# Rational layer: second product with tokens on the partitions, eight logit columns in the same product, inverse taken per block

## The chip, the cores and the metric

One core of one Trainium2 chip runs the whole program. The metric is device microseconds (us) of one execution. PE is the matrix engine, ACT, DVE and POOL the scalar, vector and general engines, SP the queue that issues most DMAs.

## What is computed

Three layers in a row on 8 × 3072 tokens of 256 channels. The first mixes along the sequence in the frequency domain; the second is the rational layer; the third routes every token to one of eight experts.

```python
# layer 2: x is the output of layer 1, 24576 x 256; w_in 256 x 2048, w_out 2048 x 256
h = x @ w_in
h2 = h * h
P = a[0] + a[1] * h + a[2] * h2 + a[3] * h2 * h
Q = 1.0 + np.abs(b[0]) * np.abs(h) + np.abs(b[1]) * h2
x = (P / (Q + 1e-06)) @ w_out
# layer 3: 8 experts, w1 256 x 1024, w2 1024 x 256
en = expert_emb / (norm(expert_emb) + 1e-06)
logits = (x / (norm(x) + 1e-06)) @ en.T / tau
e = argmax(logits); gate = softmax(logits)[e]
out = gate * (relu(x @ w1[e]) @ w2[e])
```

## The kernel before

Each layer is a stage. A planner (`list_order`, L83) simulates the engines with the costs of a table and writes one fixed order per engine: every engine then works off its list strictly in turn. Stage 1 and stage 2 have a list each.

**Stage 1** (`dft_phase`, L166) goes through 8 batches of 13 groups as matrix products. PSUM gives it two banks `pa`, shared by the first transform (`a_mm`, L264) and the last (`o_mm`, L412). Beside it run the `weight_steps` (L234): 32 chunks of `w_in` and `w_out` are read as float64, rebuilt on DVE (`w_bits`, L597 to 612) and split into a high and a low float32r part (`w_high`, `w_left`, `w_low`), which go back to DRAM (`w_hl`). Small `side` tasks (L879) prepare the coefficients and put the normed expert embeddings and two identities into `rt` (`en_turn`, L894).

**Stage 2** (`moe1_phase`, L934) has 96 tiles of 256 tokens. A tile is eight blocks; a block is 256 of the 2048 hidden channels as two halves of 128, for 256 tokens: 128 × 512 values. Per block:

- `pe_h` (L1000): 12 matmuls (two halves, three products of high and low parts, two halves of the 256 inputs) into one of six PSUM banks `h`; channels on the partitions, tokens along the row.
- `act_hb`, `act_h2`, `act_w` (L1009, L1012, L1019) and `dve_q`, `dve_m` (L1015, L1026) make Q and part of P. `Q` and `r0` hold two blocks in a row of 1024.
- `act_y0`, `act_r0` (L1030, L1033): 1/Q as the square of an inverse root, in place, for a pair of blocks in one instruction of 1024; it waits for both blocks' Q.
- `dve_g` (L1037) gives the high part `gh`; `pool_q` (L1041), `dve_rho` (L1045) and `pool_gl` (L1052; on DVE for one block in eight) the low part `gl`. `dve_rho` gives the bank `h` back.
- `pe_o` (L1062): 12 matmuls with `w_out` as the stationary operand and 256 tokens moving; the eight blocks of a tile add up in one bank `po`, channels on the partitions.

At the end of a tile `x2` (L1091, ACT) scales `po` into SBUF, `tok` (L1107, L1109) multiplies by `rt` twice to put tokens on the partitions and to make the logits (128 + 8 + 128 columns), in an `h` bank, and `tokc` (L1114, ACT) copies that out. Every 6 tiles (last batch 6, 4 and 2) `route1` to `route3` find each token's expert, and `scatter` (L1173, L1174, POOL) writes the rows to DRAM by expert. `pe_o` of the next tile's first block waits for `x2`.

**Stage 3** (`moe2_phase`, L1296) gathers 512 rows of one expert at a time and does the two products (L1482, L1498).

The names that the change touches: `COST`, `BUFS`, `SHIFT` (L213 to 231: the planner's costs, buffer counts and shifts of due times), `weight_steps`, `side`, and in stage 2 `wo`, `buffer`, `pe_o`, `x2`, `tok`, `tokc`, `all_tasks`.

Of the kernel before, what the change touches and what calls it, by code (L numbers as in the profile page):

```python
# [11 lines left out]
F32 = mybir.dt.float32  # L12
F32R = mybir.dt.float32r
# [152 lines left out]
def dft_phase(ctx, tc, io, ab, ub, xt_hl, area, side, fill, early):  # L166
# [361 lines left out]
    for name, key in order:  # L528
# [18 lines left out]
COST = {"act": 478, "act_b": 571, "act_p": 947, "dve": 602, "dve_s": 663, "pool": 1225, "pe": 1306, "tok": 461,  # L547
        "tokc": 271, "route1": 1702, "route2": 300, "route3": 2147, "dma": 1038, "scatter": 1130, "plan": 900, "ai": 852}
# [3 lines left out]
BUFS = {"h": (6, "pe"), "h2": (1, "act"), "hb": (2, "act"), "Q": (3, "dve"), "w": (2, "act"), "r0": (3, "act"),  # L552
        "qg": (3, "pool"), "pr": (3, "dve"), "gh": (5, "dve"), "gl": (4, "pool"), "x": (2, "act"),
        "rows": (2, "pe"), "po": (1, "pe")}
# [5 lines left out]
    "act_h2": -4962, "act_hb": -6207, "act_r0": 3459, "act_w": (14430, 14357), "act_y0": -2013, "ai": -970,  # L560
    "ai_h": 3981, "ai_l": -9377, "dve_g": (-3461, -2997), "dve_gl": -5717, "dve_m": (5161, 2346), "dve_q": -4054,
    "dve_rho": (-7574, 5025), "load_wo": 9288, "load_xt": -112, "pe_h": (-664, -1624), "pe_o": (-590, -4780),
    "pool_gl": -176, "pool_q": (-7749, -6544), "prepare": -896, "route1": -2684, "route2": -611, "route3": -7781,
    "scatter": 1107, "tok": -5517, "tokc": -1691, "x2": -5776,
# [3 lines left out]
def weight_steps(nc, task, work, w64, w_in, w_out, w_hl, flip, ready):  # L568
# [9 lines left out]
    whl = work.tile([128, 2, 256], F32, name="whl")  # L578
# [35 lines left out]
    def w_high(q):  # L614
        nc.scalar.copy(whl[:, 0, :].bitcast(F32R), tf)

    def w_left(q):
        V.tensor_tensor(out=tf, in0=tf, in1=whl[:, 0, :], op=ALU.subtract)

    def w_low(q):  # L620
        V.tensor_tensor(out=whl[:, 1, :].bitcast(F32R), in0=tf, in1=uf, op=ALU.add)

    def w_store(q):
        if q < 16:
            dst = w_hl[0].rearrange("p (h c) -> p h c", h=2)[:, :, 256 * q:256 * q + 256]
        else:
            dst = w_hl[1, :, 512 * (q - 16):512 * (q - 15)].rearrange("p (h c) -> p h c", h=2)
        nc.sync.dma_start(out=dst, in_=whl)

    for n, q in enumerate([*range(16, 32), *range(16)]):  # L630
        s = 5 + 2.85 * n
# [90 lines left out]
def moe1_setup(tc, io, small, area, w_hl, xt_hl, xs, cap):  # L722
# [156 lines left out]
    def side(task, sb):  # L879
# [25 lines left out]
        task(en_load, "en", "sp", 500, [("b_mm", (1, 2))], (), ("u",), step=s - 1)  # L905
# [28 lines left out]
def moe1_phase(ctx, tc, io, c, area, w_hl, xt_hl, xs, cap):  # L934
# [13 lines left out]
    rt, itau, up, ones, ids, carry = c.rt, c.itau, c.up, c.ones, c.ids, c.carry  # L948
# [3 lines left out]
    wo = const.tile([128, 2 * NF, 2, 256], F32R, name="wo")  # L952

    def load_wo(i):
        f = slice(4 * i, 4 * i + 4)
        nc.gpsimd.dma_start(out=wo[:, f], in_=w_hl[1].rearrange("p (f h d) -> p f h d", h=2, d=256)[:, f])
# [12 lines left out]
    def buffer(tag, i):  # L969
# [4 lines left out]
        m = 12 * ROW if tag == "rows" else 1024 if tag in ("Q", "r0") else 512  # L974
# [9 lines left out]

    for tag in sorted(BUFS, key=lambda t: t not in ("rows", "x")):
        bufs[tag] = [buffer(tag, i) for i in range(BUFS[tag][0])]

# [26 lines left out]
    def dve_q(s):  # L1014
        V.scalar_tensor_tensor(out=pair("Q", s), in0=sb("h2", s), scalar=1.0 + 1e-6, in1=sb("hb", s), op0=ALU.add,  # L1015
                               op1=ALU.add)
# [73 lines left out]
    def x2(tt):  # L1090
        nc.scalar.activation(sb("x", tt), bufs["po"][0], AF.Copy, scale=c.r_x)  # L1091

# [116 lines left out]
    def all_tasks():  # L1209
# [6 lines left out]
        for s in range(steps):  # L1216
            tt, f = divmod(s, NF)
            k, e = kind(s), s - s % 2
# [10 lines left out]
            task(dve_q, s, "dve", "dve", d("act_h2", "act_hb"), [("dve_q", e)] if s > e else [], () if s > e else ("Q",),  # L1229
# [23 lines left out]
            task(pe_o, s, "pe", "pe", [gl(s)] + d("dve_g") + od, last("pe_o"), (), ("gh", "gl"), step=s)  # L1253
# [348 lines left out]
```

## Time and profile before

| | |
|---|---|
| median of 3 runs | 4308.51 us (4300.82 to 4319.66) |
| profiled execution | 4307.57 us, its span 4305.8 us |
| busy in the span | PE 4163.1 (97%), DVE 3545.4 (82%), ACT 3205.4 (74%), POOL 2559.7 (59%) |
| granted clock of PE, mean | 0.987 of 2.4 GHz |

A busy time counts an instruction from its start to its end. Matmuls and vector instructions overlap their neighbours on the same engine, so that what one costs its engine is the distance from its start to the next one's start. float32 matmuls stand as two records, float32r as one.

### The profile page before, as it was taken

Reading aid. Unit: us, or ns where it says so; the run is one execution under the profiler, and the core shown is the slowest. Engines: PE = TensorE matmul, PEld = TensorE weight load, DVE = VectorE, ACT = ScalarE, POOL = GpSimd, SP = SyncE. Lnnn points to the kernel's source line nnn. Section 1 sums busy time; section 2 is a strip of 40 time slices with the busy share of each in tenths; the row PEclk is TensorE's granted clock in tenths of the full one; section 3 lists DMA queues with packets and bytes.
Section 4 is the critical chain, followed back from the end, with each engine's and each line's share of the span. In section 5 each row is a group of like instructions: output and inputs, shape, how many; then the busy total and the mean of one; then the engine's idle time right before and its main releaser. Section 6 shows DMA issues by size and latency. Waiting matters only on the chain. (4 is left out here: it accounts for less than half of the span.)

```text
span 4305.8 us, 85307 instructions
## 1 busy us (share of the span) xinstructions
PE 4163.1 (97%) x31444; PEld 3970.5 (92%) x31444; DVE 3545.4 (82%) x6999; ACT 3205.4 (74%) x5893; POOL 2559.7 (59%) x2408
## 2 busy tenths in 40 slices
PE   7899999899999999999999999999799999999999
PEld 5788888799999999999999999999789999999998
DVE  5998888699999999999999999999766666666666
ACT  4555555699999999999999999999655555555555
POOL 2333334488889888988899889988811111111111
PEclk9999999899999999999999999999899999999999
DMA  7678886600001010100100010111144444444443
GB/s 253 226 265 268 295 266 209 221 31 31 33 31 45 31 34 31 44 33 32 42 34 34 31 41 34 34 35 37 35 166 146 133 137 147 133 137 142 135 135 113
DMA packets 221830, 458.64 MB, mean 107 GB/s; under 512 B 19424, under 2 KB 134616, under 8 KB 213972
## 3 DMA queue, kind: packets, MB, share of 16 engines
q1 hardware_dynamic: 194084, 342.37, 24.1%
q0 software_dynamic: 26880, 110.66, 7.4%
q8 instruction: 251, 4.11, 0.4%
q14 instruction: 183, 1.50, 0.1%
q10 hardware_dynamic: 432, 0.00, 0.0%
HBM read 286.98 MB, written 167.02 MB: 105 GB/s over the span
## 5 line engine op out<-in xcount | busy, mean ns | idle before, releaser
L1041 POOL TENSOR_TENSOR qg<-Q,gh 128x512 f32<-128x512 f32 x768 | 980.1, 1296 | 125.4 <-DVE gh L1037 118.2
L1062 PE MATMUL po<-gh,wo 128*128 128x256 f32 x6144 | 992.7, 284 | 0.4 <-DVE gh L1037 0.4
L1052 POOL TENSOR_TENSOR gl<-pr,r 128x512 fp32r<-128x512 f32 x672 | 861.3, 1297 | 77.2 <-ACT r L1033 36.1
L1062 PEld LDWEIGHTS po<-gh,wo 128*128 128x128 f32 x6144 | 837.3, 189 | 0.7 <-DVE gh L1037 0.7
L1505 POOL DMA_INDIRECT out_dram<-y,ids x200 | 205.8, 1029 | 976.0 <-ACT y L1504 591.8
L1062 PE MATMUL po<-gl,wo 128*128 128x256 f32 x3072 | 616.1, 282 | 8.0 <-POOL spacer L1173 5.2
L1000 PE MATMUL h<-m_area_xt,m_area_wi 128*128 128x256 f32 x4608 | 615.7, 285 | 7.4 <-DMA m_area_wi<-w_hl 5.7
L1015 DVE SCALAR_TENSOR_TENSOR Q<-h,d_outer_b 128x512 f32<-128x512 f32 x768 | 526.8, 686 | 89.8 <-ACT h L1012 85.2
L1000 PE MATMUL h<-xt,m_area_wi 128*128 128x256 f32 x4608 | 594.4, 280 | 0.2 <-DVE pr L1045 0.2
L1000 PEld LDWEIGHTS h<-m_area_xt,m_area_wi 128*128 128x128 f32 x4608 | 578.6, 192 | 8.8 <-DMA m_area_wi<-w_hl 6.6
L1037 DVE SCALAR_TENSOR_TENSOR gh<-h,r 128x512 fp32r<-128x512 f32 x768 | 507.1, 685 | 69.4 <-ACT r L1033 68.7
L1000 PEld LDWEIGHTS h<-xt,m_area_wi 128*128 128x128 f32 x4608 | 559.9, 188 | 0.4 <-DVE pr L1045 0.4
L1009 ACT ACTIVATE d_outer_b<-h 128x512 f32<-128x512 f32 x768 | 461.9, 601 | 125.7 <-PE h L1000 119.4
L1012 ACT ACTIVATE h<-h 128x512 f32<-128x512 f32 x768 | 462.6, 602 | 27.8 <-DVE Q L1015 26.7
L1062 PEld LDWEIGHTS po<-gl,wo 128*128 128x128 f32 x3072 | 473.7, 189 | 8.7 <-POOL spacer L1173 5.6
L1045 DVE SCALAR_TENSOR_TENSOR pr<-h,qg 128x512 f32<-128x512 f32 x672 | 459.2, 685 | 16.9 <-POOL qg L1041 16.2
L1482 PE MATMUL ph<-e_area_x,w1h 128*128 128x512 f32 x1600 | 443.8, 394 | 7.7 <-DVE hl L1488 4.7
L1498 PE MATMUL py<-w2h,hh 128*128 128x256 f32 x1600 | 450.6, 282 | 0.0
L1498 PE MATMUL py<-w2l,hh 128*128 128x256 f32 x1600 | 447.5, 280 | 0.0
L1498 PE MATMUL py<-w2h,hl 128*128 128x256 f32 x1600 | 446.9, 279 | 0.4 <-DVE hl L1488 0.4
L1487 ACT ACTIVATE hh<-ph 128x512 fp32r<-128x512 f32 x400 | 239.6, 599 | 262.4 <-PE ph L1482 262.4
L1030 ACT ACTIVATE r<-Q 128x1024 f32<-128x1024 f32 x384 | 406.8, 1059 | 5.8 <-DVE Q L1015 5.7
(270 smaller groups left out, 8754.5 us busy)
## 6 DMA issues: line engine op xcount, KB each, us to landing
e_area_w<-in_moe_w_dram SPq DMA_DIRECT2D x104, 1024.0 KB, 5.6
xt_hl<-o SPq DMA_DIRECT2D x84, 512.0 KB, 4.6
e_area_xr<-xs SPq DMA_DIRECT2D x52, 544.0 KB, 5.3
ab<-d_inner_a SPq DMA_DIRECT2D x48, 512.0 KB, 5.6
d_outer_su<-ub SPq DMA_DIRECT2D x48, 512.0 KB, 7.8
m_area_xt<-xt_hl POOLq DMA_DIRECT2D x24, 1024.0 KB, 5.6
xt<-xt_hl POOLq DMA_DIRECT2D x24, 1024.0 KB, 5.2
d_outer_l<-ab SPq DMA_DIRECT2D x96, 240.0 KB, 4.1
```

The costliest lines, as they stand in the source:

```text
L1000: nc.tensor.matmul(p[:, TT * e:TT * e + TT], lhsT=w[:, k, c0:c0 + 128], rhs=q[:, hl, k, :], start=(e == 0 and i == 0), stop=(i == 5), skip ...
L1009: nc.scalar.activation(sb("hb", s), sb("h", s), AF.Abs, scale=c.r_b0)
L1012: nc.scalar.activation(sb("h2", s), sb("h", s), AF.Square, scale=c.r_sb1)
L1015: V.scalar_tensor_tensor(out=pair("Q", s), in0=sb("h2", s), scalar=1.0 + 1e-6, in1=sb("hb", s), op0=ALU.add, op1=ALU.add)
L1030: nc.scalar.activation(sb("r0", s), sb("Q", s), AF.Abs_reciprocal_sqrt)
L1037: V.scalar_tensor_tensor(out=sb("gh", s), in0=sb("h", s), scalar=1.0 if fast else a0, in1=pair("r0", s), op0=ALU.add, op1=ALU.mult)
L1041: nc.gpsimd.tensor_tensor(out=sb("qg", s), in0=pair("Q", s), in1=sb("gh", s).bitcast(F32), op=ALU.mult)
L1045: V.scalar_tensor_tensor(out=h if kind(s) == "V" else sb("pr", s), in0=h, scalar=1.0 if fast else a0, in1=sb("qg", s), op0=ALU.add, op1=AL ...
L1052: nc.gpsimd.tensor_tensor(out=sb("gl", s), in0=sb("pr", s), in1=pair("r0", s), op=ALU.mult)
L1062: nc.tensor.matmul(po[:, TT * d:TT * d + TT], lhsT=w[:, p, 128 * d:128 * d + 128], rhs=v[:, TT * e:TT * e + TT], start=(f + e + i + d == 0 ...
L1482: nc.tensor.matmul(p, lhsT=w[:, k, 128 * f:128 * f + 128], rhs=v[:, k, :], start=(i == 0), stop=(i == 5))
L1498: nc.tensor.matmul(p, lhsT=h[:, c], rhs=w[:, f, :], start=(f == 0 and i == 0), stop=(f == 7 and i == 2))
```

## The change

The second product is turned round: `gh` and `gl` become the stationary operand, 128 tokens at a time, and `w_out` moves, so that tokens lie on the partitions at once. `wo` gets eight more columns per half, `w_out` times the expert embeddings, in the middle (128 + 8 + 128 = 264). Stage 1 makes these columns for each of the 16 chunks of `w_out`: turn the chunk (`e_turn`, two transposes), copy it (`e_put`), multiply with the embeddings (`e_mm`), split into two parts (`e_parts`), all in one bank `pa`. `x2` and `tok` fall away, `tokc` scales and copies straight from `po`, which is now two banks, one for each 128 tokens; `h` has five. The inverse (`act_y0`, `act_r0`) is taken for each block by itself, with 4 `Q` and 5 `r0` of 512. The side tasks come earlier, and the planner's tables are new, so that all lists of stages 1 and 2 differ.

```diff
-COST = {"act": 478, "act_b": 571, "act_p": 947, ..., "pe": 1306, "tok": 461, "tokc": 271, ...}
+COST = {"act": 478, "act_b": 571, "act_p": 500, ..., "pe": 1424, "pe_o": 1463, "tokc": 290, ...}
-BUFS = {"h": (6, "pe"), ..., "Q": (3, "dve"), "r0": (3, "act"), ..., "x": (2, "act"), "rows": (2, "pe"), "po": (1, "pe")}
+BUFS = {"h": (5, "pe"), ..., "Q": (4, "dve"), "r0": (5, "act"), ..., "rows": (2, "act"), "po": (2, "pe")}
 SHIFT = {
-    "act_h2": -4962, ..., "load_wo": 9288, ..., "scatter": 1107, "tok": -5517, "tokc": -1691, "x2": -5776,
+    "act_h2": -12840, ..., "load_wo": 13636, ..., "scatter": 5137, "tokc": -761,
...
+    def e_turn(key):
+        p = sb("pa", key)
+        for k in range(2):
+            nc.tensor.transpose(p[:, 128 * k:128 * k + 128], tf[:, 128 * k:128 * k + 128], rt[:, 0, 0:128])
+
+    def e_put(key):
+        V.tensor_copy(sb("u", key)[:, 0:256], sb("pa", key)[:, 0:256])
+
+    def e_mm(key):
+        p, t = sb("pa", key), sb("u", key)
+        for k, en in enumerate((rt[:, 0, 128:136], rt[:, 1, 0:8])):
+            nc.tensor.matmul(p[:, 256:264], lhsT=t[:, 128 * k:128 * k + 128], rhs=en, start=(k == 0), stop=(k == 1),
+                             skip_group_check=True)
+
+    def e_parts(key):
+        p = sb("pa", key)[:, 256:264]
+        V.tensor_copy(whl[:, 0, 128:136].bitcast(F32R), p)
+        V.tensor_tensor(out=whl[:, 1, 128:136].bitcast(F32R), in0=p, in1=whl[:, 0, 128:136], op=ALU.subtract)
...
-        s = 5 + 2.85 * n
+        s = 8 + 2.8 * n
...
+        if q >= 16:
+            k = ("we", q)
+            task(e_turn, k, "pe", 240, [("w_bits", (q, 5))] + turned, (), ("pa",), step=s)
+            task(e_put, k, "dve", 340, [("e_turn", k)], (), ("u",), step=s)
+            task(e_mm, k, "pe", 470, [("e_put", k)], (), (), (("u", k),), step=s)
+            task(e_parts, k, "dve", 200, [("e_mm", k), ("w_high", q)], (), (), (("pa", k),), step=s)
+            with_e = [("e_turn", k), ("e_parts", k)]
+        task(w_left, q, "dve", 335, [("w_high", q), ("w_bits", (q, 6))] + with_e[:1], step=s)
...
-        s = NG + 3
-        task(fills_d, 0, "dve", 700, [("b_mm", (1, 3))], step=s)
+        s = 6
+        task(fills_d, 0, "dve", 700, [("b_mm", (0, 5))], step=s)
...
-    wo = const.tile([128, 2 * NF, 2, 256], F32R, name="wo")
+    wo = const.tile([128, 2 * NF, 2, 264], F32R, name="wo")
...
     def pe_o(s):
...
-                for d in range(2):
-                    nc.tensor.matmul(po[:, TT * d:TT * d + TT], lhsT=w[:, p, 128 * d:128 * d + 128],
-                                     rhs=v[:, TT * e:TT * e + TT], start=(f + e + i + d == 0),
+                for j in range(2):
+                    nc.tensor.matmul(bufs["po"][j][:, 0:264], lhsT=v[:, TT * e + 128 * j:TT * e + 128 * j + 128],
+                                     rhs=wo[:, 2 * f + e, p, :], start=(f + e + i == 0),
...
-    def x2(tt):
-        nc.scalar.activation(sb("x", tt), bufs["po"][0], AF.Copy, scale=c.r_x)
...
-    def tok(tt, j):
...
-        nc.scalar.copy(rows[g][:, 2 * (tt - 12 * b - t0) + j, 0:264], sb("h", (tt, j))[:, 0:264])
+        nc.scalar.activation(rows[g][:, i, 0:264], bufs["po"][j][:, 0:264], AF.Copy, scale=c.r_x)
...
-            if s > e:
-                task(act_y0, e, "act", "act_p", [("dve_q", e), ("dve_q", s)], (), ("r0",), step=s)
-                task(act_r0, e, "act", "act_p", [("act_y0", e)], step=s)
+            task(act_y0, s, "act", "act_p", d("dve_q"), (), ("r0",), step=s)
+            task(act_r0, s, "act", "act_p", d("act_y0"), step=s)
...
-            od = [("x2", tt - 1)] if f == 0 and tt else []
+            od = [("tokc", (tt - 1, j)) for j in range(2)] if f == 0 and tt else []
```

How the lists moved, at three places. Names end in the number of a buffer.

PE, stage 2, end of the 23rd tile (the last matmuls of its last `pe_o`, one `pe_h`, the first of the next tile's `pe_o`), before:

```order
L1062 MATMUL po_6978<-gh_6972,wo 128x256 x4
L1062 MATMUL po_6978<-gl_6977,wo 128x256 x2
L1000 MATMUL h_6950<-xt_6947,m_area_wi_6855 128x256 x2
L1000 MATMUL h_6950<-xt_6947,m_area_wi_6856 128x256 x2
L1000 MATMUL h_6950<-xt_6947,m_area_wi_6855 128x256 x4
L1107 MATMUL h_6951<-rt,d_outer_b 128x136
L1109 MATMUL h_6951<-rt,d_outer_b 128x136
L1062 MATMUL po_6978<-gh_6973,wo 128x256 x4
L1062 MATMUL po_6978<-gl_6974,wo 128x256 x2
```

and now:

```order
L1095 MATMUL po_7090<-wo,gl_7089 128x264
L1095 MATMUL po_7091<-wo,gl_7089 128x264
L1039 MATMUL h_7063<-xt_7059,m_area_wi_6967 128x256 x2
L1039 MATMUL h_7063<-xt_7059,m_area_wi_6968 128x256 x2
L1039 MATMUL h_7063<-xt_7059,m_area_wi_6967 128x256 x4
L1095 MATMUL po_7090<-wo,gh_7085 128x264
L1095 MATMUL po_7091<-wo,gh_7085 128x264
```

The two small products are gone; one `pe_h` still stands between the tiles, at 44 of the 95 ends of a tile (57 before), two or three at the others. `pe_o` changes bank at every matmul.

POOL, end of stage 2, before (`qg` is `pool_q`, `gl` is `pool_gl`, MEMSET and DMA are one `scatter`, of the last group but one):

```order
L1052 TENSOR_TENSOR gl_6974<-pr_6966,r_6961 128x512
L1052 TENSOR_TENSOR gl_6975<-pr_6967,r_6961 128x512
L666 IOTA pas 1x40
L1173 MEMSET spacer 128x1
L1174 DMA xs<-d_outer_su,g_dst_6986 201216x272
L1041 TENSOR_TENSOR qg_6964<-Q_6958,gh_6970 128x512
L1041 TENSOR_TENSOR qg_6965<-Q_6958,gh_6971 128x512
L1052 TENSOR_TENSOR gl_6976<-pr_6968,r_6962 128x512
```

and now, up to the first scatter of the last group:

```order
L1087 TENSOR_TENSOR gl_7088<-pr_7080,r_7074 128x512
L1087 TENSOR_TENSOR gl_7087<-pr_7078,r_7073 128x512
L1076 TENSOR_TENSOR qg_7075<-d_outer_b,gh_7081 128x512
L1076 TENSOR_TENSOR qg_7076<-Q_7067,gh_7084 128x512
L1087 TENSOR_TENSOR gl_7086<-pr_7079,r_7072 128x512
L1087 TENSOR_TENSOR gl_7089<-pr_7080,r_7071 128x512
L1076 TENSOR_TENSOR qg_7077<-d_outer_b,gh_7085 128x512
L1194 MEMSET spacer 128x1
L1195 DMA xs<-d_outer_b,g_dst_7098 201216x272
```

Before, scatters of the last group but one stood among the last blocks' `pool_q` and `pool_gl`; now all eight stand ahead of the last tile's 8 `pool_q` and 7 `pool_gl`.

PE, stage 1: the place of the second chunk of `w_out`. As a piece of the difference (the change has +):

```order
 L335 MATMUL pk_127<-wl,xsh_136 120x256 x2
 L335 MATMUL pk_127<-wh,xsl_138 120x256 x2
-L264 MATMUL pa_122<-d_inner_x,fa 128x512
-L264 MATMUL pa_121<-d_inner_x,fa 128x512
+L638 MATMUL pa_121<-rt,wt 128x128 x2
 L299 MATMUL px_123<-d_outer_b,d_outer_l 128x240
 L301 MATMUL px_123<-d_outer_b,d_outer_l 128x240
```

`e_turn` (L638) stands where two `a_mm` stood, and `e_mm` follows ten rows later, after a `b_mm` and an `i_mm`; both `a_mm` are put elsewhere.

## Rows read from the trace of the kernel before

**Rows 1.** Busy time by stretch: us, each engine's busy us (instructions), clock, DMA share, GB/s

```profile
300.00:600.00 300.00, 279.12 (x1863) 249.09 (x1862) 267.82 (x493) 170.53 (x384) 118.39 (x127) 0.99 0.83 274
1000.00:2900.00 1900.00, 1900.00 (x16090) 1899.30 (x16089) 1739.27 (x2892) 1748.63 (x2809) 1717.22 (x1569) 1.00 0.10 35
3081.00:3127.00 46.00, 20.20 (x115) 18.18 (x113) 25.52 (x65) 9.46 (x19) 25.54 (x36) 0.66 0.26 91
```

**Rows 2.** Groups by line, 1000 to 2900 us: count, busy us, mean ns, idle before

```profile
L1107 PE MATMUL h<-rt,d_outer_b 128*128 128x136 f32 x322 | 63.5, 278 | 0.0
```

**Rows 3.** PE in order of time, end of a tile: start, us, instruction

```profile
1680.42 1.59 PE L1000 MATMUL h<-m_area_xt,m_area_wi 128*128 128x256 f32 x12
1681.85 0.40 PE L1107 MATMUL h<-rt,d_outer_b 128*128 128x136 f32 x2
...
1682.23 0.73 PE L1062 MATMUL po<-gh,wo 128*128 128x256 f32 x4
1682.79 0.41 PE L1062 MATMUL po<-gl,wo 128*128 128x256 f32 x2
```

**Rows 4.** The chain that ended last, stage 3: start, us, work

```profile
3175.12 0.88 PE pt L1447 x8
3176.00 8.48 PE py L1498 x72
3184.48 11.00 PE ph L1482 x48
```

**Rows 5.** POOL in order of time, stage 2

```profile
1668.38 2.55 POOL L1041 TENSOR_TENSOR qg<-Q,gh 128x512 f32<-128x512 f32 x2
1670.86 0.11 POOL L1173 MEMSET spacer<- 128x1 f32 x1
1671.13 1.00 POOL L1174 DMA_INDIRECT xs<-d_outer_b,g_dst  x1 [0.16 <-issue]
1672.15 1.31 POOL L1052 TENSOR_TENSOR gl<-pr,r 128x512 fp32r<-128x512 f32 x1
```

**Rows 6.** One block from its product on: PE, DVE, DVE (its partner), ACT, DVE

```profile
1667.56 1.60 PE L1000 MATMUL h<-m_area_xt,m_area_wi 128*128 128x256 f32 x12
1670.32 0.69 DVE L1015 SCALAR_TENSOR_TENSOR Q<-h,d_outer_b 128x512 f32<-128x512 f32 x1 [0.62 <-ACT h L1012]
1674.61 0.68 DVE L1015 SCALAR_TENSOR_TENSOR Q<-h,d_outer_b 128x512 f32<-128x512 f32 x1
1676.49 1.05 ACT L1030 ACTIVATE r<-Q 128x1024 f32<-128x1024 f32 x1
1678.33 1.05 ACT L1033 ACTIVATE r<-r 128x1024 f32<-128x1024 f32 x1
1679.28 0.59 ACT L1012 ACTIVATE h<-h 128x512 f32<-128x512 f32 x1
1679.79 0.68 ACT L1019 ACTIVATE w<-h,co 128x512 f32<-128x512 f32 x1
1681.87 0.69 DVE L1045 SCALAR_TENSOR_TENSOR pr<-h,qg 128x512 f32<-128x512 f32 x1
```

**Rows 7.** PE in order of time, end of stage 2, with the idle time before

```profile
3086.79 0.51 PE L1062 MATMUL po<-gl,wo 128*128 128x256 f32 x2 [1.22 <-POOL spacer L1173]
...
3091.29 0.50 PE L1062 MATMUL po<-gl,wo 128*128 128x256 f32 x2 [2.81 <-POOL gl L1052]
...
3100.33 0.80 PE L1062 MATMUL po<-gl,wo 128*128 128x256 f32 x2 [4.01 <-POOL spacer L1173]
...
3104.34 0.63 PE L1062 MATMUL po<-gl,wo 128*128 128x256 f32 x2
...
3109.92 0.19 PE L1147 MATMUL h<-g_ohb,up 128*128 128x32 bf16 x1 [2.09 <-DVE g_ohb L1139]
```

**Rows 8.** Waits, 300 to 600 us: who waited for whom, us, times, longest

```profile
PEld pa L412 <- DVE o L421: 10.5, 7, 3.4
```

**Rows 9.** Groups by line, whole span

```profile
L894 PE MATMUL pa<-rt,u 8*128 8x8 f32 x2 | 0.5, 270 | 5.3 <-DVE u L890 5.3
```

More of the change, by code (lines that the diff above doesn't have):

```diff
@@ L542 @@
 KINDS = "PPPPPPPVPPPPPPPV"
-COST = {"act": 478, "act_b": 571, "act_p": 947, "dve": 602, "dve_s": 663, "pool": 1225, "pe": 1306, "tok": 461,
-        "tokc": 271, "route1": 1702, "route2": 300, "route3": 2147, "dma": 1038, "scatter": 1130, "plan": 900, "ai": 852}
+COST = {"act": 478, "act_b": 571, "act_p": 500, "dve": 602, "dve_s": 663, "pool": 1225, "pe": 1424, "pe_o": 1463,
+        "tokc": 290, "route1": 1702, "route2": 300, "route3": 2147, "dma": 1038, "scatter": 1130, "plan": 900, "ai": 852}
 LATENCY = {"pe": {"pe": 0, "act": 197, "dve": 196, "pool": 200}, "act": {"pe": 270, "act": 143, "dve": 152, "pool": 170},
@@ L559, with weight_steps @@
 SHIFT = {
[L560 to L564, printed above, removed]
+    "act_h2": -12840, "act_hb": -6207, "act_r0": 6362, "act_w": (14430, 14357), "act_y0": 4164, "ai": -17166,
+    "ai_h": 3981, "ai_l": -15930, "dve_g": (-894, -2997), "dve_gl": -13828, "dve_m": (4781, 2346), "dve_q": -4054,
+    "dve_rho": (-7297, 3208), "load_wo": 13636, "load_xt": 975, "pe_h": (-664, -647), "pe_o": (-590, -4780),
+    "pool_gl": 916, "pool_q": (-7749, -6680), "prepare": -896, "route1": 2701, "route2": -1893, "route3": -473,
+    "scatter": 5137, "tokc": -761,
 }
-def weight_steps(nc, task, work, w64, w_in, w_out, w_hl, flip, ready):
+def weight_steps(nc, task, work, sb, w64, w_in, w_out, w_hl, flip, ready, rt, turned):
     V = nc.vector
@@ L577, in weight_steps, with part @@
     tf, uf = t.bitcast(F32), u.bitcast(F32)
-    whl = work.tile([128, 2, 256], F32, name="whl")
+    whl = work.tile([128, 2, 272], F32, name="whl")
+    split = lambda a: a.rearrange("p (k c) -> p k c", k=2)
+    def part(q, i):
+        if q < 16:
+            return whl[:, i, :256], lambda a: a
+        return whl[:, i, :].rearrange("p (k c) -> p k c", c=136)[:, :, 0:128], split
     raw = lambda q: (w64[:, q % 2, :, 0], w64[:, q % 2, :, 1])
@@ L983, in buffer @@
         return t.rearrange("p (a c) -> p a c", a=12) if tag == "rows" else t
-    for tag in sorted(BUFS, key=lambda t: t not in ("rows", "x")):
+    for tag in sorted(BUFS, key=lambda t: t != "rows"):
         bufs[tag] = [buffer(tag, i) for i in range(BUFS[tag][0])]
@@ L1014, in dve_q @@
     def dve_q(s):
-        V.scalar_tensor_tensor(out=pair("Q", s), in0=sb("h2", s), scalar=1.0 + 1e-6, in1=sb("hb", s), op0=ALU.add,
+        V.scalar_tensor_tensor(out=sb("Q", s), in0=sb("h2", s), scalar=1.0 + 1e-6, in1=sb("hb", s), op0=ALU.add,
                                op1=ALU.add)
@@ L1260, in all_tasks @@
                 after_ai = [("ai_l", key) for key in late] if first and g == groups[6] else []
-                task(tok, (tt, j), "pe", "tok", [("x2", tt)] + after_ai + ([("tokc", (tt, j - 1))] if j else []), (),
-                     ("h", "rows") if first else ("h",), (("x", tt),) if j == 1 else (), step=s + 3 * j + 2)
-                task(tokc, (tt, j), "act", "tokc", [("tok", (tt, j))], (), (), ("h",), step=s + 3 * j + 2)
+                task(tokc, (tt, j), "act", "tokc", [("pe_o", s)] + after_ai, [("tokc", (tt, 0))] if j else [],
+                     ("rows",) if first else (), (), step=s + 1)
             if tt == 12 * g[0] + g[1] + g[2] - 1:
@@ L1283, in put @@
         for name, key in order:
-            if name in ("tok", "tokc", "scatter"):
+            if name in ("tokc", "scatter"):
                 fns[name](*key)
```

75 lines of the change are left out of this document (32 added, 43 removed).

## The prediction

> **What bounds the kernel now.** I read first the busy times by stretch, to see which engine has no idle time in which stage; then PE's own order of time, because a matmul's record is longer than what it costs; then the other engines' order of time, to see how much of a tile they need; last the waits, where PE does stand still.
>
> In the middle of stage 2 PE is busy for 1900.00 of 1900.00 us at a granted clock of 1.00, while DVE (1739), ACT (1749) and POOL (1717) each have some 8 to 10% left [rows 1]. So stage 2 lasts as long as its matmuls, and these are what is to be counted. The stretch holds 322 records of the first small product, four to a tile (two products, two records each), so 80.5 tiles of 23.60 us [rows 2]. Twelve matmuls of 256 columns go by in 1.43 us, 0.119 us each [rows 3]; in stage 3 a 256-column one costs 8.48 / 72 = 0.1178 us and a 512-column one 11.00 / 48 = 0.2292 us [rows 4]. At the end of stage 2, and in stage 1, PE waits for others: 20.20 busy us of 46, and 279 of 300 [rows 1].
>
> **The small products removed.** One `tok` (L1107 and L1109) takes PE from 1681.85 to 1682.23, 0.38 us, and the four matmuls behind it then take 0.56 us where four cost 0.48: together 0.46 us [rows 3]. There are 192, two to a tile: 88 us, all of it on PE's path, where nothing hides it.
>
> **Eight more columns.** The rows of 256 and 512 columns give (0.2292 - 0.1178) / 256 = 0.435 ns a column [rows 4], so 3.5 ns for eight. With 96 `pe_o` matmuls a tile that is 0.33 us, and 32 us in all 9216. Ends: 0.119 x 8 / 256 = 3.7 ns if the whole cost grows in proportion (34 us), and nothing. That 128 + 8 columns are no second pass, the small products themselves show: four records of 136 columns pass in 0.46 us, and plain ones of 128 cost 0.88 / 8 = 0.11 us each [rows 3, 4]. The weight loads stay 96, of 128 columns. The Trainium skill, TensorE: Matmul & The Clock Gate, section Back-to-back issue gap, gives a sustained 81 ns for 128 columns and 131 ns for 512, by which eight columns would add about 1.0 ns each (an estimate from that page), 10 us in place of 32, and the time would be 22 us below my forecast. The rows disagree with it here: 229 ns for 512 columns.
>
> So a tile becomes 23.60 - 0.92 + 0.33 = 23.01 us, and 96 tiles give **-56 us**. Ends: -39 (0.38 for a `tok`, 34 us added) and -88.
>
> **Whether the others keep up.** ACT: an instruction of 1024 costs 0.95 us from its start to the next start, one of 512 0.51 [rows 6]; eight of the first and `x2` (as one of 512) are 8.1 us a tile, sixteen of 512 are 8.2. Nothing changes. POOL: two products in 2.48 us, a scatter in 1.29 [rows 5]; 15 and 2 of these are 21.2 us a tile, 92% of 23.01. The five banks `h`: in the block shown the product ends at 1669.16 and `dve_rho`, which frees its bank, at 1682.56, 13.4 us. Of this its Q, done at 1671.01, waits until 1675.29 for the partner's (4.3), and both inverse steps cost 0.44 more than at 512 [rows 6]. Taken block by block that is 8.2 us; five banks at 2.88 us a block allow 5 x 2.88 - 1.43 = 13.0. That holds. End of a tile: the next `pe_o` waits for two `tokc`, with ACT's 0.51 as their bound 1.0 us, and at the least one `pe_h` of 1.43 us stands between. If ACT comes one instruction late (0.68 [rows 6]), 0.3 us at 44 ends shows, 13 us; I count nothing.
>
> **Ends of stage 2.** At its end PE waited 1.22, 2.81 and 4.01 us for POOL, the first and last behind a scatter, and from the last `pe_o` (3104.97) to the first routing product (3109.92) `x2`, two `tok` and two `tokc` go by, 2.09 us of it routing on DVE [rows 7]. The scatters now stand ahead, the inverse waits for no partner, and of the 2.9 us of copies only the two `tokc` are left: I take 6 of 8.0 and 2 of 2.9, **-8 us** (ends -2 and -10). At its start the list is new as well, with the first `pe_o` earlier; the nearest stretch with waits is the 8.0 us just named, so 0, with ends -8 and +8.
>
> **Stage 1.** Sixteen chunks get two transposes (0.11 each [rows 4]) and two small float32 products, priced as one `tok`, 0.46 (an upper bound by the nearest row): 0.68 us, 10.9 in all. PE stands still for 21 of 300 us there [rows 1], so most of it shows: **+10**. The copy and the two small splits on DVE lie beside other work, but PE's list stands behind `e_mm` until DVE has copied, and the chunk holds one of two banks `pa` meanwhile. `o_mm` already waits for that bank, 10.5 us in 7 waits, 1.5 each [rows 8]; one such wait for each chunk would make 10.9 + 24 = 35, the upper end. The lower end is -5: the embeddings' transposes, now in batch 0, made PE wait 5.3 us [rows 9]. Stores and loads grow by 8 columns in 256, which I count as nothing.
>
> **Sum.** -56 - 8 + 10 = -54 us on the profiled execution's 4307.6 us: **4254 us**. The median of the runs shown is 0.9 us higher than that execution; I leave this out.
>
> **Rivals.** About 0.5% (21.5 us) is what a measurement of this kernel can tell from no change.
>
> *POOL's list becomes the bound.* POOL was idle for 183 of 1900 us, 2.3 us a tile [rows 1], and would have 1.8. If its in-order list needs all of the 2.3, a tile stays at 23.6 and only the ends count: 4307.6 - 8 + 10 = 4310. If half of the gain goes, 4282. For it speaks that the three other engines, at 90 to 92% busy, all rise by 2.5% at once; against it, that PE had not one visible wait in 1900 us [rows 1].
>
> *The fifth bank decides (slower).* With one bank `h` fewer, PE's next product waits until `dve_rho` has freed the oldest. It decides above 13.0 us from the product to `dve_rho`, and the block shown took 13.4 [rows 6]. Above 13.45 us the kernel is slower by 0.5%: a block then costs (13.45 + 1.43) / 5 = 2.98 us, a tile 23.8. At 13.8 us a tile takes 24.4, and the kernel 4254 + 130 = 4384. PE standing still also costs its clock: in the stretch with the waits of 2.81 and 4.01 us it was 0.66, so partly at 1.2 GHz [rows 1, 7]. The Trainium skill, TensorE: Matmul & The Clock Gate, section A second HAM failure mode: psum-queue depth-cycling, tells of a kernel whose cycling through PSUM banks made PE pause so often that the clock swung; the trace does not agree so far, as six banks are cycled at a clock of 1.00. Against this rival speaks the 8.2 us worked out above.
>
> *Stage 1 pays more.* With 35 instead of 10: 4279.
>
> *Columns cost less.* With 10 us for the eight columns in place of 32: 4231.
>
> **How the numbers follow.** Forecast 4254 (4236 to 4275 by its own bounds): 0.62. Stage 1 at 4279: 0.09. POOL with half of the gain gone, 4282: 0.06; with all gone, 4310: 0.12. Fifth bank, 4384: 0.08. Columns, 4231: 0.03. Faster by over 0.5% (below 4287) are the first, second, third and last: 0.80; within 0.5% the 4310: 0.12; slower 0.08. The range 4228 to 4290 leaves out the 4310 and the fifth bank, 0.20.
>
> **What would show it.** Right: in the middle of stage 2 PE busy throughout at a clock of 1.00, a tile of about 23.0 us, twelve 264-column matmuls in 1.46 us, no float32 matmul between blocks, and in the chain or the waits no bank `h`. ACT's inverse rows at 512 with a start every 0.51 us. At the end of stage 2 no wait of PE behind a scatter, and stage 1 about 10 us longer. Wrong: idle time before `pe_h` ended by `dve_rho` (the fifth bank), idle before `pe_o` ended by POOL or by `tokc`, a clock below 1.00 in the middle of stage 2, or a stage 1 longer by more than 35 us.

## The result, and the profile after

The kernel became slower: 4373.38 us in the median (4370.37 to 4374.98) against 4312.45 (4300.82 to 4319.66), ratio 1.0145, 95% interval 1.0132 to 1.0157. The profiled executions span 4373.3 and 4305.8 us, 67.5 apart:

| stretch, us | before | after | predicted (+ and - are differences) |
|---|---|---|---|
| start to first `pe_h` | 785.4 | 787.9 | +10 |
| first `pe_h` to end of last `pe_o` | 2319.6 | 2389.5 | -62 |
| of it the first two tiles | 72.9 | 84.0 | 0 |
| of it a tile, mean of tiles 6 to 89 | 23.65 | 24.35 | 23.01 |
| of it last `pe_h` to last `pe_o`, ends | 21.5 | 9.8 | shorter by 6 |
| last `pe_o` to the end of the span | 1200.8 | 1195.9 | -2 |

(A tile is taken from the start of its first `pe_h` to that of the next tile.) So the loss lies in the middle of stage 2, with 11 us more in its first two tiles. The busy times by stretch, after, which answer to [rows 1] (us, PE, PEld, DVE, ACT, POOL, clock, DMA share, GB/s):

```profile
300.00:600.00 300.00, 277.57 (x1864) 247.63 (x1863) 268.28 (x506) 168.15 (x378) 117.51 (x125) 0.99 0.82 273
1000.00:2900.00 1900.00, 1831.44 (x15018) 1805.21 (x15017) 1725.60 (x2811) 1719.92 (x3277) 1667.02 (x1521) 1.00 0.10 34
```

PE, which had no gap before, now stands idle for 69 us of the 1900, at a granted clock of 1.00, and all other engines do less than before as well: everybody waits for somebody. The matmuls themselves are what was predicted. PE in order of time, after, which answers to [rows 3]:

```profile
1682.66 1.56 PE L1039 MATMUL h<-xt,m_area_wi 128*128 128x256 f32 x12
1684.05 0.64 PE L1095 MATMUL po<-wo,gh 128*128 128x264 f32 x4
1684.53 0.41 PE L1095 MATMUL po<-wo,gl 128*128 128x264 f32 x2
1684.78 0.65 PE L1095 MATMUL po<-wo,gh 128*128 128x264 f32 x4
1685.27 0.40 PE L1095 MATMUL po<-wo,gl 128*128 128x264 f32 x2
1685.51 0.64 PE L1095 MATMUL po<-wo,gh 128*128 128x264 f32 x4
```

Twelve of 264 columns go by in 1.46 us (1684.05 to 1685.51). In the median one stands 0.1215 us before the next, one of 256 columns 0.118, so a tile is 96 x 0.2395 = 22.99 us of matmuls. The other 24.35 - 22.99 = 1.36 us are stalls, 131 us in 96 tiles. Who waited for whom, 1000 to 2900 us, after (us, times, longest):

```profile
ACT r L1065 <- DVE d_outer_b L1050: 127.5, 89, 4.2
POOL qg L1076 <- DVE gh L1072: 124.2, 104, 3.2
...
PE h L1039 <- DVE pr L1080: 26.8, 47, 1.7
...
PE h L1168 <- DVE g_ohb L1160: 22.4, 13, 1.8
...
PE h L1039 <- DVE gl L1084: 11.6, 11, 1.6
```

ACT, POOL and PE all wait for DVE. L1168 is `route2`: 13 routing groups, one every sixth tile, 1.7 us each. The mean tile by its place in a period of twelve shows the same: 24.6 and 25.7, then four of 23.1 to 24.0, then 26.2 and 26.0, then four of 23.4 to 24.6; the four longest are those in which a routing runs (`route1` and `route2` in the first and the seventh, `route3` in the second and the eighth). So that is where to look. DVE in order of time at one routing, after:

```profile
1713.57 1.18 DVE L1150 TENSOR_SCALAR g_d<-d_outer_su,itau 128x96 f32<-128x96 f32 x1
1714.68 1.33 DVE L1151 TENSOR_SCALAR d_outer_su<-ids 128x96 f32<-128x96 f32 x1
1715.93 0.24 DVE L1153 TENSOR_REDUCE g_m<-g_d 128x12 f32<-128x96 f32 x1
1716.21 1.09 DVE L1154 TENSOR_TENSOR g_d<-g_d,g_m 128x96 f32<-128x96 f32 x1
1717.33 0.26 DVE L1156 TENSOR_TENSOR g_d<-g_d,wexp 128x96 f32<-128x96 f32 x1
...
1718.20 0.24 DVE L1160 CAST g_ohb<-g_d 128x96 bf16<-128x96 f32 x1
1718.37 0.68 DVE L1080 SCALAR_TENSOR_TENSOR pr<-h,qg 128x512 f32<-128x512 f32 x1
```

POOL in the same time, after:

```profile
1713.38 1.32 POOL L1076 TENSOR_TENSOR qg<-d_outer_b,gh 128x512 f32<-128x512 f32 x1
1714.62 2.56 POOL L1087 TENSOR_TENSOR gl<-pr,r 128x512 fp32r<-128x512 f32 x2
1719.22 1.28 POOL L1087 TENSOR_TENSOR gl<-pr,r 128x512 fp32r<-128x512 f32 x1 [2.03 <-DVE pr L1080]
```

And PE, after:

```profile
1715.11 1.58 PE L1039 MATMUL h<-m_area_xt,m_area_wi 128*128 128x256 f32 x12
1718.50 0.20 PE L1168 MATMUL h<-g_ohb,up 128*128 128x96 bf16 x1 [1.81 <-DVE g_ohb L1160]
...
1719.10 1.65 PE L1039 MATMUL h<-m_area_xt,m_area_wi 128*128 128x256 f32 x7 [0.36 <-DVE pr L1080]
```

Three small DVE steps take over a microsecond each, and each ends just behind the end of a POOL product: L1150 at 1714.75 (product 1714.70), L1151 at 1716.01 (the first of the two products ends at 1715.95), L1154 at 1717.30 (the second at 1717.18). The reduction between them, L1153, takes 0.24. The same lines before, grouped (behind the bar: us in all, mean ns):

```profile
L1129 DVE TENSOR_SCALAR g_d<-d_outer_su,itau 128x96 f32<-128x96 f32 x7 | 9.3, 1333 | 0.0
...
L1133 DVE TENSOR_TENSOR g_d<-g_d,g_m 128x96 f32<-128x96 f32 x13 | 3.4, 259 | 0.4
...
L1130 DVE TENSOR_SCALAR d_outer_su<-ids 128x96 f32<-128x96 f32 x7 | 1.4, 198 | 0.0
```

Before, only the first of the three stood behind a product, since POOL then waited for ACT. POOL at such a routing before, where the step of L1129 runs from 1687.12 to 1688.45:

```profile
1685.85 2.54 POOL L1041 TENSOR_TENSOR qg<-Q,gh 128x512 f32<-128x512 f32 x2
1690.97 2.54 POOL L1052 TENSOR_TENSOR gl<-pr,r 128x512 fp32r<-128x512 f32 x2 [2.58 <-ACT r L1033]
```

L1156, after, met no product either. It is the same at each of the 13 routings in the stretch: L1154 always begins during a product and takes 1.09 us, where its twin before, L1133, never does and takes 0.26. `route1` took 3.0 us before and takes 4.8 and 4.1 in turn after, and the list reckons with 1.70 in both.

### The profile page after: what moved, and what is told of

Its sections match the earlier page's. It is cut to its first block, busy times and chain, and to the rows that moved or that the text cites. A ratio compares the mean times of both kernels' runs of the same rounds, so it can differ in the third digit from the quotient of the medians.

```text
span 4373.3 us, 84825 instructions
## 1 busy us (share of the span) xinstructions
PE 4152.4 (95%) x30772; PEld 3928.4 (90%) x30772; DVE 3586.5 (82%) x7047; ACT 3230.6 (74%) x6565; POOL 2560.0 (59%) x2408
## 5 line engine op out<-in xcount | busy, mean ns | idle before, releaser
L1095 PE MATMUL po<-wo,gh 128*128 128x264 f32 x6144 | 1004.0, 285 | 1.3 <-ACT d_outer_su L1135 0.3
L1095 PEld LDWEIGHTS po<-wo,gh 128*128 128x128 f32 x6144 | 851.3, 189 | 5.2 <-ACT d_outer_b L1135 3.1
L1076 POOL TENSOR_TENSOR qg<-d_outer_b,gh 128x512 f32<-128x512 f32 x576 | 742.9, 1297 | 159.6 <-DVE gh L1072 155.5
L1095 PE MATMUL po<-wo,gl 128*128 128x264 f32 x3072 | 625.8, 285 | 4.6 <-DVE gl L1084 3.4
L1061 DVE SCALAR_TENSOR_TENSOR h<-w,co,h 128x512 f32<-128x512 f32 x768 | 566.0, 748 | 32.2 <-ACT w L1054 30.1
L1054 ACT ACTIVATE w<-h,co 128x512 f32<-128x512 f32 x768 | 528.3, 702 | 3.9 <-DVE h L1061 3.4
L1068 ACT ACTIVATE r<-r 128x512 f32<-128x512 f32 x768 | 486.8, 643 | 7.0
L1095 PEld LDWEIGHTS po<-wo,gl 128*128 128x128 f32 x3072 | 478.9, 189 | 7.8 <-DVE gl L1084 5.0
L1065 ACT ACTIVATE r<-d_outer_b 128x512 f32<-128x512 f32 x576 | 370.4, 643 | 146.8 <-DVE d_outer_b L1050 143.1
L1050 DVE SCALAR_TENSOR_TENSOR d_outer_b<-h,d_outer_b 128x512 f32<-128x512 f32 x576 | 394.4, 685 | 74.9 <-ACT d_outer_b L1044 60.6
```

What stands on the lines that cost most here:

```text
L1054: nc.scalar.activation(sb("w", s), sb("h", s), AF.Square if fast else AF.Identity, scale=c.r_sa, bias=ca)
L1061: V.scalar_tensor_tensor(out=h, in0=sb("w", s), scalar=ka, in1=h, op0=ALU.add, op1=ALU.mult)
L1068: nc.scalar.activation(sb("r0", s), sb("r0", s), AF.Square)
L1076: nc.gpsimd.tensor_tensor(out=sb("qg", s), in0=sb("Q", s), in1=sb("gh", s).bitcast(F32), op=ALU.mult)
L1095: nc.tensor.matmul(bufs["po"][j][:, 0:264], lhsT=v[:, TT * e + 128 * j:TT * e + 128 * j + 128], rhs=wo[:, 2 * f + e, p, :], start=(f + e + ...
```

## The experiments

Theory A: the routing's DVE steps stand still behind POOL's products, and DVE's lateness reaches PE, because every other engine would be over 90% busy in the shorter tile. A2: the list is besides written for a POOL that is too quick. B: five banks are too few. C: the inverse block by block, or the second product's form, costs. D: the list lost its reserve when PE's cost was made exact. E: a better list is worth the same with either kernel. "Replaying the list" in the expectations is an estimate: each instruction, in the order written out, starts when its engine and all that it waits for are done, with durations from the two traces (`pe_h` 1.418, `pe_o` 1.458, a POOL product 1.252, a scatter 1.30 us and so on). For the two kernels it gives 23.8 and, with `route1` at its mean of 4.43, 24.35 us a tile, where 23.65 and 24.35 were measured. Ratios are to the kernel before, run in the same round (its medians there lie between 4305.6 and 4308.2); the changed kernel's is 1.0145. Two kernels with other costs or shifts have other lists. e14 shows what that alone can do, so a small difference between two lists proves little.

| run | us | ratio (95%) | a tile |
|---|---|---|---|
| e1: routing out of POOL's way | 4346.9 | 1.0087 (1.0068 to 1.0105) | 24.03 |
| e2: POOL's costs corrected | 4322.3 | 1.0030 (1.0016 to 1.0043) | 23.66 |
| e3: PE's costs low | 4406.3 | 1.0217 (1.0195 to 1.0239) | 24.56 |
| e4: e1 and e2 | 4284.7 | 0.9941 (0.9918 to 0.9964) | 23.28 |
| e5: before, five banks | 4414.7 | 1.0240 (1.0216 to 1.0264) | 24.75 |
| e6: six banks, `h2` in SBUF | 4756.4 | 1.1032 (1.1007 to 1.1058) | 28.40 |
| e7: e4, shifts searched again | 4276.5 | 0.9922 (0.9907 to 0.9936) | 23.26 |
| e8: before, with e4's edits | 4361.6 | 1.0129 (1.0105 to 1.0152) | 24.23 |
| e9: before, inverse by block | 4316.0 | 1.0008 (0.9997 to 1.0019) | 23.72 |
| e10: before, shifts searched | 4316.4 | 1.0020 (1.0008 to 1.0031) | 23.78 |
| e13: before, POOL's costs | 4344.1 | 1.0086 (1.0064 to 1.0108) | 24.00 |
| e14: shifts moved by chance | 4334.9 | 1.0060 (1.0043 to 1.0077) | 23.86 |

**e1.** The main lines:

```diff
-        d = tiles["d"].rearrange("p (t e) -> p t e", e=NE)[:, :n, :]
+        d = sb("h", g)[:, 96:192].rearrange("p (t e) -> p t e", e=NE)[:, :n, :]
...
-        V.tensor_scalar(out=r[:, :n, 264:272], scalar1=float(b * 3072), scalar2=None, op0=ALU.add,
+        nc.scalar.activation(r[:, :n, 264:272], func=AF.Copy, bias=float(b * 3072),
...
-                task(route1, g, "dve", "route1", [("tokc", (tt, 1))], step=p)
+                task(route1, g, "dve", "route1", [("tokc", (tt, 1))], (), ("h",), step=p)
```

> The changed kernel with one edit: what route1 and route3 keep between their steps (d, tot) lies in the PSUM bank that route2 takes anyway, taken by route1 already; the column of token numbers is written by ScalarE, the mask is copied once before stage 2. The costs and shifts that order the work are those of the change. Theory A (VectorE's routing steps wait for GpSimd): in the changed kernel's trace L1150, L1151 and L1154 take 1.18, 1.33 and 1.09 us where the same steps took 1.33, 0.20 and 0.26 us before, and each ends some 0.1 us after a GpSimd product ends. Without it route1 falls from 4.8 to about 2.0 us and route3 from 3.3 (mean) to 2.5, 16 times: 58 us less of VectorE, and since every engine is over 92% busy there, nearly all of it reaches TensorE. Expected 4316 us (4300 to 4335), the waits before the first pe_h block after a routing and before route2 shorter by half. Theory B (five banks are too few): a bank is now held for 3 us longer in every group, so 4373 to 4385. Theory C (the inverse block by block, or the second product's new form): no change, 4373.

4346.9, above the 4300 to 4335 expected: 26 us of the 57. e1's lists are those of the changed kernel: the planner gives every engine the same tasks in the same order, so these 26 us come from the shorter routing and not from another list. They lie where `route1` is: in the period of twelve, the first and the seventh tile fall from 24.6 to 22.9 and from 26.2 to 23.8, and no other moves by 0.4. PE's wait before `route2`, 22.4 us above, is gone. `route1` fell to 2.01 us in every full group, `route3` to 2.5 and 3.1 in turn. Groups by line of e1 (behind the bar: us in all, mean ns):

```profile
L1184 DVE COPY carry<-g_inc 128x8 f32<-128x8 f32 x13 | 6.4, 492 | 0.4
...
L1157 DVE TENSOR_TENSOR h<-h,g_m 128x96 f32<-128x96 f32 x13 | 3.5, 266 | 0.5
...
L1153 DVE TENSOR_SCALAR h<-d_outer_su,itau 128x96 f32<-128x96 f32 x7 | 2.2, 317 | 0.0
```

With one operand in PSUM the same steps take 0.27 to 0.32 us beside POOL's products; the copy of 8 columns from SBUF to SBUF (L1184) now meets them instead, at every second routing. DVE has 2.7 us less a routing, not 3.6: I had taken 4.8 for every `route1`, and `route3` gave 0.3 in place of 0.8. A bank held longer did not turn the sign; what a bank is worth e1 does not say.

**e2, e3, e4.**

```diff
-COST = {"act": 478, "act_b": 571, "act_p": 500, "dve": 602, "dve_s": 663, "pool": 1225, "pe": 1424, "pe_o": 1463,
-        "tokc": 290, "route1": 1702, "route2": 300, "route3": 2147, "dma": 1038, "scatter": 1130, "plan": 900, "ai": 852}
+COST = {"act": 478, "act_b": 571, "act_p": 500, "dve": 602, "dve_s": 663, "pool": 1252, "pe": 1424, "pe_o": 1463,
+        "tokc": 290, "route1": 1702, "route2": 300, "route3": 2147, "dma": 1038, "scatter": 1300, "plan": 900, "ai": 852}
```

That is e2; e3 has `"pe": 1306, "pe_o": 1343` instead, e4 the edits of e1 and e2.

> The changed kernel with two numbers of the order's costs corrected to what the trace shows: pool 1225 to 1252, scatter 1130 to 1300. Nothing that is computed changes, only the order. Theory A2 (the order was written for a GpSimd that is 3% faster than it is: 15 products and 2 scatters a tile make 22.0 us of GpSimd where the costs say 20.6, and so the list asks GpSimd for results too early): an estimate by replaying the list with the trace's durations gives 23.9 us a tile in place of 24.4, or 4322 us (4305 to 4345). Theories B and C: the order is another one of the same quality, 4365 to 4380.

> The changed kernel with TensorE's costs as low as they were before the change in proportion (pe 1424 to 1306, pe_o 1463 to 1343). Nothing that is computed changes, only the order. Theory D (the order before was written for a TensorE 9% faster than it is, which left every other engine slack; the change took that slack away with its exact costs): 4310 to 4340. Theory A (what is late is VectorE's routing and GpSimd, whatever TensorE is planned at): no gain; the replayed list gives 24.7 us a tile, 4394 us (4370 to 4410).

> The changed kernel with the edits of the first two together: the routing out of GpSimd's way, and GpSimd's costs as measured. Theories A and A2 together: the replayed list gives 23.3 us a tile, 4263 us (4245 to 4290), below the kernel before (4305 to 4312). Theory B: not below 4330, since the five banks are left as they are and one is held longer. Theory C: not below 4330, since the inverse and the second product are left as they are.

(In the first the 22.0 should read 21.4: 15 x 1.252 + 2 x 1.30.) Theory D foretold 4310 to 4340; the one list written for a quicker PE is 33 us slower than the changed kernel, so D has nothing for it. e2 ends in A2's range, e4 in that of both, 89 us below the changed kernel and 23 below the one before, with the number of banks, the inverse and the second product untouched. e4's lists differ from e2's at 111 of 10511 places, so nearly all of the 38 us between the two is the routing's again. The middle of stage 2 in e4, in the columns above:

```profile
1000.00:2900.00 1900.00, 1885.10 (x15702) 1874.47 (x15701) 1758.47 (x2906) 1803.90 (x3444) 1753.65 (x1600) 1.00 0.11 36
```

**e14** asks whether e2 needed those costs. Two of the shifts that it moves:

```diff
-    "dve_rho": (-7297, 3208), "pe_h": (-664, -647),
+    "dve_rho": (-7288, 3202), "pe_h": (-656, -654),
```

> The changed kernel with its costs as they are and 22 of its 24 shifts moved by up to 13 units (10 units are one block), by chance; nothing that is computed changes. It asks whether the 51 us of e2 need GpSimd's corrected costs, or whether another order with the old costs gives as much. Of 60 such sets this is the one whose list, replayed with the trace's durations, ends first: 23.9 us a tile, 38 us less than the changed kernel's own list, 4335 us (4315 to 4360). If only corrected costs help (A2 alone): 4365 to 4385.

4334.9, 38 us less with the old costs, as the replay had it. So e2's 51 us show what the order is worth, and not that POOL's costs were the reason: 38 of them came with the best, by replay, of 60 lists that chance made. In replays of 30 sets, with the shifts moved by 5 units (standard deviation), the corrected costs end 40 us earlier in the mean, with a spread of 20 us among the sets. In a second such series they end earlier in each of 30 sets, by 19 to 58 us. Both are estimates; no run shows what the costs by themselves are worth.

**e5.** In the kernel before:

```diff
-BUFS = {"h": (6, "pe"), "h2": (1, "act"),
+BUFS = {"h": (5, "pe"), "h2": (1, "act"),
```

> The kernel before with five h banks in place of six, nothing else edited; the order is written anew by the same costs. Theory B (a bank decides): the prediction's own point was a chain from the product to dve_rho of 13.45 us, and before it is 13.1 in the median and up to 15.9 with pairs; replaying the list with the trace's durations gives 24.9 a tile in place of 23.8, or 4305 + 110 = 4415 us (4380 to 4440). If banks are not scarce at all: 4300 to 4320. What it says of the changed kernel is that there the chain is 11.5 us in the median, so that the same loss would have to be looked for elsewhere.

One bank fewer costs 2.4% where the inverse goes by pairs, with the list that the planner writes for it. PE's wait there is the same one as in the changed kernel (waits of e5, 1000 to 2900 us):

```profile
PE h L1000 <- DVE pr L1045: 34.1, 52, 1.5
```

**e6.** In the changed kernel:

```diff
-BUFS = {"h": (5, "pe"), "h2": (1, "act"),
+BUFS = {"h": (6, "pe"), "h2": (1, "act"),
...
-        if tag in ("h", "h2", "po"):
+        if tag in ("h", "po"):
```

> The changed kernel with h2 in SBUF, which makes its PSUM bank the sixth h bank. Theory B: with six banks the chain has 2.9 us more, and the stalls before pe_h go: 4310 to 4360. Theory A (VectorE's steps that read two tiles in SBUF stand still while a GpSimd product runs): dve_q now reads two SBUF tiles, h2 and hb, where one lay in PSUM, and waits for the rest of a GpSimd product (half of 1.25 us on average) 768 times. Its occupancy goes from 0.60 to about 1.1 us, VectorE from 20.3 to 24.3 us a tile plus the routing, above TensorE's 23.1: 27 us a tile by the replayed list, 4600 us (4500 to 4700).

Slower still than expected, with a sixth bank. DVE in e6:

```profile
1698.60 1.49 DVE L1050 SCALAR_TENSOR_TENSOR Q<-d_outer_b 128x512 f32<-128x512 f32 x1
...
1701.93 0.68 DVE L1050 SCALAR_TENSOR_TENSOR Q<-d_outer_b 128x512 f32<-128x512 f32 x1
...
1706.18 3.15 DVE L1050 SCALAR_TENSOR_TENSOR d_outer_b<-d_outer_b 128x512 f32<-128x512 f32 x1
```

and POOL there:

```profile
1699.50 1.74 POOL L1076 TENSOR_TENSOR qg<-Q,gh 128x512 f32<-128x512 f32 x1
...
1701.43 1.01 POOL L1195 DMA_INDIRECT xs<-d_outer_b,g_dst  x1
...
1706.22 2.55 POOL L1087 TENSOR_TENSOR gl<-pr,r 128x512 fp32r<-128x512 f32 x2
```

A Q takes 0.68 us beside a scatter and 3.15 beside two products, all of both; its mean is 1.27 where it was 0.68. What a sixth bank is worth without this was not tried, since the eight PSUM banks are all given out; the replay puts it at 13 us in the changed kernel and at nothing with e4's costs and routing (estimates). That e4 and e7 come to a tile of 23.3 with five banks shows that five do not force the 24.35.

**e7.** The kernel of e4 with other shifts, among them:

```diff
-    "route1": 2701, "route3": -473, "scatter": 5137, "pool_gl": 916,
+    "route1": -29606, "route3": 25851, "scatter": 22179, "pool_gl": 10065,
```

> The kernel of e4 (the changed kernel with the routing out of GpSimd's way and GpSimd's costs as measured) with the shifts that order the list searched again for the least end by the trace's durations. Theory A with A2: the columns and the banks allow 23.0 to 23.1 us a tile as predicted, and what held the changed kernel above it was the list; 23.1 a tile, 4262 us (4248 to 4276). Theory B or C: no list helps, not below 4284.

4276.5, just above its range, 32 us below the kernel before and 97 below the changed one; the tile is 23.26, not 23.1. It is the fastest of all. What PE still loses lies at the routing: the first two of each six tiles have stalls of 0.3 to 1.4 us, the other four next to none.

**e8, e10, e13.** The kernel before with the edits of e1 and e2, with other shifts alone, and with e2's costs alone:

```diff
-    "route1": -2684, "route2": -611, "route3": -7781,
+    "route1": 37280, "route2": -609, "route3": -17802,
```

These are three of e10's shifts.

> The kernel before with the same two edits as e4: the routing out of GpSimd's way (its PSUM bank taken by route1 already) and GpSimd's costs as measured. If the edits of e4 are what made it fast, whatever the change (theory E), they help here as well: 4220 to 4290. Theory A: before, TensorE has no wait in the middle of stage 2, so there is nothing for them to give; the list is another one, with a bank held longer, and the replayed list gives 24.2 us a tile in place of 23.8: 4343 us (4315 to 4365).

> The kernel before with the shifts of its list searched in the same way and for as long as in e7. Theory E (a searched list is worth as much to either kernel, about 90 us): 4215 to 4260. Theory A: TensorE is busy throughout with 23.6 us of matmuls a tile, which no list shortens; the search found 8 us: 4300 us (4288 to 4315).

> The kernel before with GpSimd's costs corrected as in e2 (pool 1252, scatter 1300), nothing else. Theory E: faster by 30 to 50 us, as in e2. Theory A: no gain, since TensorE had no waits; the shifts were found for the other costs, and the replayed list gives 24.0 us a tile in place of 23.8, 4325 us (4305 to 4340).

Theory E fails three times: none makes that kernel faster. (e10 and e13 ended a few us above their ranges.) PE's matmuls hold it, and these three lists only added waits: of 1900 us PE was busy for 1900.0 before and for 1873.5, 1895.3 and 1882.7 here. So the gain of e4 and e7 belongs to the changed kernel.

**e9.** In the kernel before, with the cost `act_p` at 500 and `pair` taken out of all its users:

```diff
-"Q": (3, "dve"), "w": (2, "act"), "r0": (3, "act"),
+"Q": (4, "dve"), "w": (2, "act"), "r0": (5, "act"),
...
-            if s > e:
-                task(act_y0, e, "act", "act_p", [("dve_q", e), ("dve_q", s)], (), ("r0",), step=s)
-                task(act_r0, e, "act", "act_p", [("act_y0", e)], step=s)
+            task(act_y0, s, "act", "act_p", d("dve_q"), (), ("r0",), step=s)
+            task(act_r0, s, "act", "act_p", d("act_y0"), step=s)
```

> The kernel before with one part of the change alone: the inverse block by block (act_y0 and act_r0 on 512 columns, four Q and five r0 of 512), six h banks, tok, x2 and the second product as they were. Theory C (the inverse block by block costs): ScalarE pays 16 x 0.521 - 8 x 0.948 = 0.8 us more a tile, which would be up to 73 us if ScalarE were late: 4330 to 4380. Theory A: ScalarE has that room, and the shorter chain is not what is waited for: 4295 to 4320.

1.0008: in the kernel before, the inverse by block costs nothing that can be seen; in the changed kernel it was not tried by itself. That the second product's form costs no more than its columns is told by the spacing of its matmuls, 0.1215 us. e4 and e7 keep both and are faster than the kernel before, so theory C is not what made the loss.

## Why the prediction was wrong, step by step

*The small products and the columns: right.* A tile has 22.99 us of matmuls, predicted 23.01. Eight columns cost 3.5 ns (0.1215 against 0.118 us), as the rows of 256 and 512 columns had said. The Trainium skill, TensorE: Matmul & The Clock Gate, section Back-to-back issue gap, would have had 1.0 ns by its sustained figures (an estimate from that page); these runs do not agree with it.

*Whether the others keep up: this step failed.* It compared each engine's work with a tile's time (POOL at 92%) and then set the stalls to nothing; they are 1.36 us a tile, 131 us, and turn the forecast -56 of the tiles into a loss. e1's routing out of POOL's way takes 26 us of them, e4 with another list besides brings the tile to 23.28, and 0.29 us a tile, 28 in all, is left. What the step left out is that the work doesn't come evenly. Every sixth tile DVE has two routing steps, 7.5 us in the changed kernel (`route1` 4.4 and `route3` 3.1 in the mean; 3.0 and 2.9 before), and POOL twelve scatters. I had counted the scatters as a mean of two a tile, and the routing nowhere but at the end of stage 2. In the kernel before this was hidden by PE's longer tile, and how thin the cover was could have been read: over blocks 100 to 699, the bank that a product took had been given back only 0.07 us before in the closest case, and for a quarter of the blocks less than 1.39 us before (which bank a block has is in the planner's list). Those are the numbers to set against a tile that gets 0.6 us shorter, not the 183 us in which POOL was idle. After, the quarter is 0.45 us, and 110 of the 600 products start within 0.1 us of their bank's return, where 6 did.

*The five banks, "That holds": half right.* From product to `dve_rho` there are 11.5 us in the median (13.1 before), below the 13.0 allowed, but not the 8.2 worked out; 22% of the blocks are above 13.0, up to 18.3. The sign I had named for the fifth bank, PE idle before `pe_h` until `dve_rho`, is there, but it doesn't tell the cause by itself: the banks are also the place where any lateness of DVE reaches PE. e1 took a third of a routing's DVE time away, held a bank for longer, and 26 us went.

*The rivals.* POOL's list was the nearest in kind and ended at 4310, because I let the tile grow back to 23.6 and no further. Nothing sets that limit: an engine that comes late can cost more than was won. The fifth bank, at 4384 with a tile of 24.4, came within 11 us of the result, but by luck: its condition was 13.8 us from product to `dve_rho` at every block, and the median is 11.5. The clock that I feared for with it stayed at 1.00 in the middle of stage 2 (in e6, where PE was busy for 1652 of 1900 us, it was 0.96).

*The ends.* Stage 2's end won more than the 8 us: 11.7 before the end of the last `pe_o`, and 2.7 from there to the first routing product. PE at the end, after, which answers to [rows 7]:

```profile
3176.20 0.52 PE L1095 MATMUL po<-wo,gl 128*128 128x264 f32 x2 [0.76 <-DVE gl L1084]
...
3177.03 0.40 PE L1095 MATMUL po<-wo,gl 128*128 128x264 f32 x2
3179.69 0.18 PE L1168 MATMUL h<-g_ohb,up 128*128 128x32 bf16 x1 [2.26 <-DVE g_ohb L1160]
```

The first two tiles cost 11 us more, outside the ends of -8 and +8; why was not looked into. Stage 1 cost 2.5, not 10: its new matmuls, by line, after, are

```profile
L646 PE MATMUL pa<-rt,u 128*128 128x8 f32 x64 | 8.4, 240 | 0.7 <-DVE u L641 0.7
L638 PE MATMUL pa<-rt,wt 128*128 128x128 f32 x32 | 6.9, 298 | 4.5 <-DVE wt L616 3.8 <-ACT d_inner_a L272 0.8
```

and most of that lay in waits that PE had anyway: up to the first `pe_h` its busy time grew by 9.3 us (699.3 to 708.6), the time by 2.5.

What stays open: which part of e2's gain is due to POOL's costs, the worth of a sixth bank, the first two tiles, and the 0.3 us a tile that e4 and e7 still lose.

## What to carry to other kernels

An engine that is busy throughout hides the lateness of all others. When a change makes it faster, the price of what it hid is read from the reserve of the buffers (how long before its use each was free, the lower quarter and the least) and from the work that comes in bursts, not from shares of busy time. An order written out by costs holds for one set of costs: with the same work, lists here lay 84 us apart (4406 to 4322), so a changed kernel is judged only with a list of its own, and the old one beside it with as good a list. A rival in which an engine "becomes the bound" has no ceiling at the old time.

## What the hardware showed

In these runs DVE and POOL shut each other out. A DVE step that reads two SBUF tiles, or a copy or scalar step from SBUF to SBUF, ended about 0.1 us behind a running POOL product, and so took up to 1.3 us in place of 0.2 to 0.3; it stood through two products on end (3.15 us, e6), and a POOL product begun at 1699.50 was drawn out to 1.74 us, while a Q from 1698.60 ran until 1700.09. A reduction (0.24), steps with one operand in PSUM (0.27) and steps beside a scatter (0.68 for a Q) were not held up. The Trainium skill, SBUF — State Buffer, section Who interferes with whom, says that the two engines share a pair of ports, which one has alone for a whole instruction, and names steps with two SBUF inputs, and copies or scalar steps from SBUF to SBUF, among those that take part; these runs agree. That a waiting step can be passed by the next product, as in e6, it does not say. That `h2` lies in PSUM here is thus worth more than a sixth bank: e6, which trades the one for the other, is 383 us slower than the changed kernel.
